# Five heads to two loads: K and V rows of 160 tokens in an eight-megabyte ring, against rows of 128 tokens for two heads

## The chip, the cores and the metric

The kernel runs on one core of one Trainium2 chip. The metric is the device time of that core in microseconds, the median of several executions. TensorE is called PE, VectorE DVE, ScalarE ACT, GpSimd POOL and SyncE SP, as in the profile; PEld is PE's weight load. SP issues the loads.

## The reference

Two attention blocks, A and B, each decode one token for a batch of 2 with 32 heads of 192 dimensions over a cache of 8192 tokens:

```python
q = (x @ wq).reshape(B, Sq, Hq, Dh).transpose(0, 2, 1, 3)     # x: 2 x 1 x 640, wq: 640 x 6144
scores = jnp.einsum("bhqd,bhkd->bhqk", q, k) * (Dh ** -0.5)   # k: 2 x 32 x 8192 x 192
p = _softmax(scores, axis=-1)
o = jnp.einsum("bhqk,bhkd->bhqd", p, v_cache)
out = o.transpose(0, 2, 1, 3).reshape(B, Sq, Hq * Dh) @ wo    # wo: 6144 x 640
```

All tensors are bf16; the two results are concatenated. K and V of both blocks are 805 MB, the four weights 31 MB.

## The kernel before

A load of K or V brings 128 partitions of 128 tokens (49152 B each, 6144 KB in all). As a head has 8192 tokens, that is two heads: partitions 0 to 63 hold one, 64 to 127 the other. The 2 x 32 heads of a block make 32 such pairs, the two blocks `NP = 64` steps. `rings` holds three loads; K and V go through the three slots in turn (order K V K V), V of a step one step behind K.

SP (`program_sync`, L92 to L159) loads the query weights of both blocks into slots 0 and 1 and the first K into slot 2, then one K when the projection of block A is done (`pr`), one V when that of B is, and from there one load after the other. Each waits for an earlier load of its kind to have landed and for PE to have used up what lies in its slot (`pv` counts value matmuls, `su` score matmuls). `hold` (L82) is a wait and an increment of a counter that nothing reads. At the end it loads the output weights of A, the last V in two halves, and the output weights of B in five pieces as PE frees their rows (`ca`).

PE (L316 to L421) first projects x (`pe_first`, L395 to L419): 12 column tiles of 512 per block, two to a turn, ten matmuls; ACT copies each result to `qrow` (L278). `make_q` (L322) spreads a pair's query over all partitions through a selection matrix, and ACT copies the right half for the lower and the upper 64 partitions into `qt` (L272, L273). In the main loop (L356) each step t does: `make_q` for the next pair; the scores of pair t; `put`, which lays a finished head's output into its column of `oall` (L327); the sum of the exponentials (L379); the value matmuls of pair t-1 in four turns of 16 (L385). After the last pair but for its values, the output rows of A are computed (`rows`, L339), then the last values, then the rows of B.

Scores: DVE multiplies K by the query in place, in four parts of 32 tokens (L241); PE adds up groups of 16 of the 192 products by matmuls with the identity (48 per pair, 12 per part, L370); DVE adds the 16 sums that remain (L246) and takes the maxima of the two halves (L250, L251); POOL spreads the maxima over partitions (L191); ACT makes the bias (L296), exponentials and their sums (L302). `closing` (L222) on DVE and `gather` on ACT (L286) scale the output of the step before.

## Time and profile before

| | |
|---|---|
| time, median of 3 | 1935.83 us (1935.47 to 1935.84) |
| profiled execution, span from first to last instruction | 1934.3 us; its own time outside the span is not recorded, and the median lies 1.5 us above the span |
| bytes read | 836.77 MB, 433 GB/s over the span |
| busy: PE, DVE, ACT, POOL | 1558.2, 1075.6, 186.5, 27.9 us |
| granted clock of PE, mean | 0.965 |
| K or V load, issue to landing, median | 26.5 to 26.8 us |

The busy share of an engine is over the whole span. A PE row's duration is that of pipelined matmuls, so the starts of rows say more than their lengths. "<-issue" behind a row is time in which the engine waited for its own instruction stream and for nothing that the profile shows. In a timeline row stand the start, the length, the engine, the line, the operation with its tiles, the count of merged instructions, and in brackets the idle time before it with what ended it.

### The profile page before, as it was taken

What the parts mean: (1) busy time and instruction counts of PE and PEld (TensorE: products, weight loads), DVE (VectorE), ACT (ScalarE), POOL (GpSimd) and SP (SyncE); (2) the same over time, 40 slices, a digit from 0 to 9 for tenths busy, and PEclk for the clock granted to TensorE, in tenths of its full rate; (3) what the DMA queues carried; (4) which work ended last, traced back from release to release, by engine and by line L of the source; (5) the groups of instructions that cost most, each with busy time, mean ns of one, the idle gap of its engine ahead of it and who ended that gap; (6) DMA issues with size and microseconds to landing.
All of it is one profiled execution on the core that took longest, in us unless ns stands there. A gap on an engine that the chain in (4) does not pass through costs nothing.

```text
span 1934.3 us, 31141 instructions
## 1 busy us (share of the span) xinstructions
PE 1558.2 (81%) x7939; PEld 743.0 (38%) x7939; DVE 1075.6 (56%) x717; ACT 186.5 (10%) x598; POOL 27.9 (1%) x83
## 2 busy tenths in 40 slices
PE   5787888887888887888887888887888888888887
PEld 1343333333333333333333333333433333433434
DVE  0665565565565565565565565565565565565560
ACT  2110010010010010010010010010010010010010
POOL 1000000000000000000000000000000000000000
PEclk9899999999999999999999999999999999999999
DMA  9999999999999999999999999999999999999999
GB/s 421 425 439 439 423 439 439 425 437 439 430 432 439 431 431 439 433 429 439 435 427 439 437 425 439 437 425 439 437 425 439 439 425 437 439 430 432 439 435 394
DMA packets 19896, 836.78 MB, mean 433 GB/s; under 512 B 2220, under 2 KB 2360, under 8 KB 2744
## 3 DMA queue, kind: packets, MB, share of 16 engines
q1 hardware_dynamic: 19880, 836.78, 100.0%
q10 hardware_dynamic: 16, 0.01, 0.0%
HBM read 836.77 MB, written 0.01 MB: 433 GB/s over the span
## 4 chain that ended last, share of the span: by engine, by line
DMA 44%; PE 32%; DVE 10%; issue 10%; another core or an unknown queue 2%; DVEq 1%; SPq 0%; ACT 0%; POOLq 0%
DMA rings<-in_B_k_cache_dram 22%; DMA rings<-in_A_k_cache_dram 19%; PE ops L385 18%; PE scps L370 12%; DVE rings L241 10%; DMA rings<-in_A_wo_dram 2%; DMA rings<-in_B_wo_dram 1%; DVEq L241 1%; PE oall L327 0%; PE qps L339 0%; PE ops L379 0%; SPq L102 0%; DVE qrow L212 0%; DVE sc L246 0%
## 5 line engine op out<-in xcount | busy, mean ns | idle before, releaser
L241 DVE TENSOR_TENSOR rings<-rings,qt 128x6144 bf16 x256 | 842.5, 3353 | 722.9 <-DMA rings<-in_B_k_cache_dram 351.0
L385 PE MATMUL ops<-rings,pb 128*34 x4096 | 712.9, 327 | 166.9 <-issue 166.9
L370 PE MATMUL scps<-rings,ident 128*128 x3072 | 749.0, 403 | 105.5 <-DVE rings L241 102.6
L385 PEld LDWEIGHTS ops<-rings,pb 128*34 x4096 | 381.3, 93 | 483.0 <-issue 233.5
L370 PEld LDWEIGHTS scps<-rings,ident 128*128 128x128 bf16 x3072 | 314.5, 102 | 524.0 <-issue 249.6
L246 DVE TENSOR_REDUCE sc<-scps 128x64 f32<-128x1024 f32 x128 | 155.5, 1215 | 81.4 <-PE scps L370 81.4
L286 ACT ACTIVATE oodd<-ops 2x192 f32<-2x192 f32 x65 | 20.9, 321 | 731.4 <-PE ops L385 731.4
L272 ACT ACTIVATE qt<-qps 64x192 bf16<-64x192 f32 x65 | 21.0, 323 | 650.1 <-DVE rings L241 649.6
L302 ACT ACTIVATE pb<-sc,nb 64x128 bf16<-64x128 f32 x128 | 82.4, 644 | 2.6
L322 PE MATMUL qps<-qrow,sel 36*128 (+1 forms) x66 | 21.8, 331 | 72.4 <-issue 69.6
L296 ACT ACTIVATE nb<-mg 64x1 f32<-64x1 f32 x128 | 25.7, 201 | 302.8 <-POOL mg L191 302.1
L191 POOL PARTITION_ALL_REDUCE mg<-mp x64 | 22.7, 354 | 1856.8 <-DVE mp L251 1856.8
L322 PEld LDWEIGHTS qps<-qrow,sel 36*128 (+1 forms) x66 | 6.1, 93 | 94.0 <-issue 94.0
L302 ACT ACTIVATION_READ_ACCUMULATOR pb<-sc,nb 64x1 f32 x128 | 39.2, 306 | 0.0
L411 PE MATMUL scps<-rings,xT 128*4 x120 | 29.4, 410 | 6.3 <-POOLq L188 6.3
L224 DVE RECIPROCAL rc<-ops 2x1 f32<-2x1 f32 x66 | 9.8, 149 | 34.5 <-PE ops L385 34.5
L327 PEld LDWEIGHTS oall<-on,place 2*128 x260 | 12.5, 92 | 29.7 <-issue 29.2
L226 DVE TENSOR_TENSOR oodd<-ops,oodd 2x192 f32<-2x192 f32 x66 | 21.5, 326 | 0.4 <-ACT oodd L286 0.4
L229 DVE TENSOR_SCALAR on<-oodd,rc 2x192 bf16<-2x192 f32 x66 | 20.3, 307 | 2.3
L273 ACT ACTIVATE qt<-qps 64x192 bf16<-64x192 f32 x65 | 21.1, 325 | 0.8
L327 PE MATMUL oall<-on,place 2*128 2x48 bf16 x260 | 19.6, 183 | 1.9 <-DVE on L229 1.7
L411 PEld LDWEIGHTS scps<-rings,xT 128*4 128x4 bf16 x120 | 10.7, 89 | 24.2 <-issue 12.2
(38 smaller groups left out, 109.9 us busy)
## 6 DMA issues: line engine op xcount, KB each, us to landing
rings<-in_A_k_cache_dram SPq DMA_DIRECT2D x32, 6144.0 KB, 26.8
rings<-in_A_v_cache_dram SPq DMA_DIRECT2D x32, 6144.0 KB, 26.5
rings<-in_B_k_cache_dram SPq DMA_DIRECT2D x32, 6144.0 KB, 26.7
rings<-in_B_v_cache_dram SPq DMA_DIRECT2D x31, 6144.0 KB, 26.6
rings<-in_B_wq_dram SPq DMA_DIRECT2D x1, 7680.0 KB, 37.9
rings<-in_A_wo_dram SPq DMA_DIRECT2D x1, 7680.0 KB, 30.7
rings<-in_A_wq_dram SPq DMA_DIRECT2D x1, 7296.0 KB, 20.2
rings<-in_B_v_cache_dram SPq DMA_DIRECT2D x2, 3072.0 KB, 26.8
```

Of the source, the lines that this page charges most:

```text
L191: eng.partition_all_reduce(mg[:], mp[:], 128, bass.bass_isa.ReduceOp.max).then_inc(Z["ar"], 1)
L226: eng.tensor_tensor(oodd[:], ops[0:2, 0:Dh], oodd[:], ALU.add).then_inc(Z["dd"], 1)
L241: eng.tensor_tensor(k3, k3, q3, ALU.mult).then_inc(Z["mu"], 1)
L246: eng.tensor_reduce(sc[:, h * 2 * TQ:(h + 1) * 2 * TQ], scps[:, 2 * h:2 * h + 2, :].rearrange("p k (t g) -> p (k t) g", g=DG), AXL.X, ALU. ...
L273: eng.activation(qt[64:128, :], qps[64:128, Dh:2 * Dh], ACTF.Identity).then_inc(Z["qtd"], 1)
L296: ins = eng.activation(nb[p0:p0 + 64, :], mg[p0:p0 + 64, h:h + 1], ACTF.Identity, scale=-scale)
L302: ins = eng.activation(pb[p0:p0 + 64, :, h::32], sc[p0:p0 + 64, :].rearrange("p (j a) -> p j a", a=2), ACTF.Exp, bias=nb[p0:p0 + 64, :], s ...
L322: eng.matmul(qps[:, 0:2 * Dh], sel[:].rearrange("p s m -> p (s m)")[:, bass.ds(k, 128)], qrow[:, bass.ds(c, 2 * Dh)], start=True, stop=Tru ...
L327: ins = eng.matmul(oflat[:, bass.ds(sec, WR)], place[:, bass.ds(at - a, 128)], on[:, a * WR:(a + 1) * WR], start=False, stop=False, skip_g ...
L370: ins = eng.matmul(dst, ident[:], src[:, :, 0:DG], start=(j == 0), stop=(j == NJ - 1))
L385: ins = eng.matmul(ops[0:PW, 0:2 * Dh], pbflat[:, bass.ds(aj + j * PW, PW)], rings[:, bass.ds(vj + j * (2 * Dh), 2 * Dh)], start=False, st ...
L411: ins = eng.matmul(scflat[0:4, bass.ds(to + h * QC, QC)], xT[:, c, :], rings[:, bass.ds(at + (c * N + h * QC), QC)], start=(c == 0), stop= ...
```

## The change

A chunk is now 32 tokens of 192, 12288 B, and a partition's row is five chunks of one load (160 tokens, 61440 B). Two loads (K0, K1) hold the keys of five heads, two more (V0, V1) the values, so head boundaries fall inside a load, at other partitions and chunks than before. A block has 12 groups of five heads and one of four, whose rows are 128 tokens (four chunks); 26 groups in all, 104 loads. The ring still has three slots, now of 61440 B per partition. The order is K0 of group t, V0 of group t-1, K1 of t, V1 of t-1. Before the first V come three K loads. Each load waits for the load two places ahead to have landed and for the load three places ahead to have been used up.

As one partition can belong to different heads in different chunks, a load needs up to three query vectors per partition (`qt` has 2 x 3). ACT no longer copies the queries: DVE makes them from `qps` with masks (`low`, `high`, `take`: 24 operations per group, of 192 or 96 columns, the first of each target a product with a mask column, the others a product added to it). The projection runs in turns of one column tile, five matmuls, 14 turns per block, and both blocks are projected before the first query is made. The maximum is taken per chunk, masked per head (`MN`), spread by POOL as five columns, and turned into biases on DVE. The exponentials are up to 18 operations per group in place of two per pair. POOL forwards the landings of loads to DVE (`kd`) and PE (`vs`). Reductions now run once per load over 2560 columns. PE's score loop has a turn per chunk; `put` has a loop of two turns for the two batch rows; values take five turns of 16 matmuls per load (four in the small group). At the end both V loads of the last group, the second in two halves, stand behind the output weights of A.

The added lines, cut to the core (removed ones stand in the kernel above; indentation shortened):

```diff
+    TC = 32
+    CW = TC * Dh
+    NCH = 5
+    SCH = 4
+    HCH = Sk // TC
+    T = NCH * TC
+    NS = 5
+    GB = B * Hn // NS
+    GL = GB + 1
+    NG = NBLK * GL
+    UR = 128 * NCH
...
+    load("k", 0, 0, NCH, 2 * SW, "k0")
+    eng.wait_ge(Z["pr"], NPD)
+    load("k", 0, UR, NCH, 0, "lb")
+    eng.wait_ge(Z["pr"], 2 * NPD)
+    def step(t, kb, krow, kn, ku, vb, vrow, vn, vu):
+        val = (lambda x: x) if isinstance(t, int) else eng.snap
+        first = isinstance(t, int) and t == 1
+        s0, s1, s2 = val(t % 3 * SW), val((t + 1) % 3 * SW), val((t + 2) % 3 * SW)
+        if not first:
+            hold(eng, "la", val(t * 32 - 32))
+            hold(eng, "pv", val(t * 2))
+        load("k", kb, krow, kn, s0, "la")
+        hold(eng, "lb", val(t * 32 - 16))
+        hold(eng, "su", NCH if first else val(t * (2 * NCH)))
+        load("v", vb, vrow, vn, s1, "lb")
+        hold(eng, "la", val(t * 32 - 16))
+        if first:
+            hold(eng, "su", 2 * NCH)
         else:
+            hold(eng, "pv", val(t * 2 + 1))
+        load("k", kb, val(krow + ku), kn, s2, "la")
+        hold(eng, "lb", val(t * 32))
+        hold(eng, "su", val(t * (2 * NCH) + NCH))
+        load("v", vb, val(vrow + vu), vn, s0, "lb")
+    def both(t, blk, g):
+        step(t, blk, eng.snap(g * GR), NCH, UR, blk, eng.snap(g * GR - GR), NCH, UR)
+    step(1, 0, GR, NCH, UR, 0, 0, NCH, UR)
+    with eng.Fori(2, GB) as t:
+        both(t, 0, t)
+    step(GB, 0, GB * GR, SCH, SR, 0, (GB - 1) * GR, NCH, UR)
+    step(GL, 1, 0, NCH, UR, 0, GB * GR, SCH, SR)
+    with eng.Fori(GL + 1, NG - 1) as t:
+        both(t, 1, eng.snap(t - GL))
+    step(NG - 1, 1, GB * GR, SCH, SR, 1, (GB - 1) * GR, NCH, UR)
...
+            hold(eng, "lb", 32 * g + 16)
+            eng.wait_ge(Z["su"], 2 * NCH * (g + 1))
+            load("v", 1, GB * GR, SCH, 0, "lb")
+            eng.wait_ge(Z["pv"], 2 * g + 3)
+            src = rows_of("v", 1, GB * GR + SR, SCH)
+            for h, (a, e) in enumerate(((0, LATE * CW), (LATE * CW, SCH * CW))):
+                eng.dma_start(rings[:, SW + a:SW + e], src[:, a:e]).then_inc(vq[h], 16)
...
+    pass_on("k0", 16, "kd")
+    pass_on("lb", 16, "kd")
+    maximum(1)
+    with eng.Fori(1, NG) as t:
+        pass_on("la", eng.snap(t * 32 - 16), "kd")
+        pass_on("lb", eng.snap(t * 32), "vs")
+        pass_on("la", eng.snap(t * 32), "kd")
+        pass_on("lb", eng.snap(t * 32 + 16), "vs")
+        maximum(eng.snap(t + 1))
...
+    def multiply(at, u, c):
+        v = max(0, min(2, c - 2 * u))
+        k3 = rings[:, bass.ds(at + c * CW, CW)].rearrange("p (t d) -> p t d", d=Dh)
+        q3 = qt[:, u, v, :].unsqueeze(1).broadcast_to([128, TC, Dh])
+        eng.tensor_tensor(k3, k3, q3, ALU.mult).then_inc(Z["mu"], 1)
+    def reduce(u, upto):
+        eng.wait_ge(Z["su"], upto)
+        eng.tensor_reduce(sc[:, u, :], scps[:].rearrange("p k (t g) -> p (k t) g", g=DG),
+                          AXL.X, ALU.add).then_inc(Z["re"], 1)
+    def take(u, s, d0, d1, at, new):
+        for v in range(3):
+            dst, src, m = qt[:, u, v, d0:d1], qps[:, at:at + d1 - d0], QW[:, (u * 3 + v) * 3 + s:(u * 3 + v) * 3 + s + 1]
+            if new:
+                ins = eng.tensor_scalar(dst, src, m, None, ALU.mult)
+            else:
+                ins = eng.scalar_tensor_tensor(dst, src, m, dst, ALU.mult, ALU.add)
+        return ins
+    def low(n, w):
+        val = (lambda x: x) if isinstance(n, int) else eng.snap
+        H = Dh // 2
...
+        eng.wait_ge(Z["qk"], val(n * 2 + 1))
+        eng.wait_ge(Z["qc"], val(n * 5 + 1))
+        take(0, 0, 0, Dh, 0, True)
+        take(1, 0, 0, H, 2 * Dh, True).then_inc(Z["qc"], 1)
+        eng.wait_ge(Z["qc"], val(n * 5 + 2))
+        take(0, 1, 0, Dh, Dh, False).then_inc(Z["qc"], 1)
+        eng.wait_ge(Z["qc"], val(n * 5 + 3))
+        take(0, 2, 0, H, 2 * Dh, False).then_inc(Z["qs"], 1)
+    def high(n):
+        H = Dh // 2
+        eng.wait_ge(Z["qk"], eng.snap(n * 2 + 2))
+        eng.wait_ge(Z["qs"], eng.snap(n + 1))
+        take(1, 0, H, Dh, 0, True)
+        take(0, 2, H, Dh, 0, False).then_inc(Z["qc"], 1)
+        eng.wait_ge(Z["qc"], eng.snap(n * 5 + 4))
+        take(1, 1, 0, Dh, H, False).then_inc(Z["qc"], 1)
+        eng.wait_ge(Z["qc"], eng.snap(n * 5 + 5))
+        take(1, 2, 0, Dh, H + Dh, False).then_inc(Z["qt"], 1)
+        eng.wait_ge(Z["qt"], eng.snap(n + 1))
+    low(0, 0)
+    with eng.Fori(0, NG) as t:
+        y = eng.snap((t + 31) >> 5)
+        at = [eng.snap((t + 2 - y * 2) % 3 * SW), eng.snap((t + 3 - y) % 3 * SW)]
+        w = eng.snap(kind(t))
+        high(t)
+        eng.wait_ge(Z["kd"], eng.snap(t * 2 + 1))
+        for c in range(NCH):
+            multiply(at[0], 0, c)
+        closing(t - 2)
+        eng.wait_ge(Z["ex"], eng.snap(t * 2 + 1))
+        reduce(0, eng.snap(t * (2 * NCH) + NCH))
+        n = eng.snap(t * 4)
+        last = sc[:, 0, SCH * TC:T]
+        eng.wait_ge(Z["re"], eng.snap(t * 2 + 2))
+        eng.tensor_scalar(last, last, flag[:, bass.ds(w, 1)], None, ALU.min).then_inc(Z["ch"], 1)
+        eng.wait_ge(Z["kd"], eng.snap(t * 2 + 2))
+        for c in range(NCH):
+            multiply(at[1], 1, c)
+        low(eng.snap(t + 1), eng.snap(kind(t + 1)))
+        reduce(1, eng.snap(t * (2 * NCH) + 2 * NCH))
+        eng.wait_ge(Z["ch"], eng.snap(n + 1))
+        eng.wait_ge(Z["re"], eng.snap(t * 2 + 3))
+        eng.tensor_reduce(cm, sc[:].rearrange("p u (c t) -> p (u c) t", t=TC), AXL.X,
+                          ALU.max).then_inc(Z["ch"], 1)
...
+        eng.tensor_reduce(mp, nb[:], AXL.X, ALU.max).then_inc(Z["mx"], 1)
+        eng.wait_ge(Z["ar"], eng.snap(t + 1))
+        eng.scalar_tensor_tensor(nb[:], mg.unsqueeze(2).broadcast_to([128, NS, 2 * NCH]), -scale, mask,
+                                 ALU.mult, ALU.add).then_inc(Z["nbd"], 1)
+        eng.sem_inc(Z["ch"], 1)
...
+    def exps(u):
+        for v, (c0, c1) in enumerate(SPANS[u]):
...
+                ins = eng.activation(dst, src, ACTF.Exp, bias=nb[:, s, k:k + 1], scale=scale,
+                                     accum_out=rs[:, u, v, s:s + 1])
         ins.then_inc(Z["ex"], 1)
+    with eng.Fori(0, NG) as t:
+        eng.wait_ge(Z["nbd"], eng.snap(t + 1))
+        eng.wait_ge(Z["pv"], eng.snap(t * 2 + 2))
+        exps(0)
+        gather(t - 1)
+        exps(1)
...
+    def put(t):
+        z = eng.snap((t + 17) >> 5)
+        x = nc.snap(z * (4 * 65) - t * (4 * NS) + (P0 + 2 * 4 * NS), min_val=3, max_val=PLW - 256)
+        z = eng.snap(z * 128)
+        with eng.Fori(0, B) as b:
+            zb, xb = eng.snap(b * 64 + z), eng.snap(b * 128 + x)
+            for a in range(4):
+                ins = eng.matmul(oall[:, bass.ds(zb, WR)], place[:, bass.ds(xb - a, 128)],
+                                 on[:, a * WR:(a + 1) * WR], start=False, stop=False,
+                                 skip_group_check=True)
+            ins.then_inc(Z["pl"], 1)
...
+        with eng.Fori(eng.snap(p * NG), eng.snap(p * 2 + NG)) as t:
+            with eng.Fori(0, 2) as u:
+                with eng.If(t < NG):
+                    y = eng.snap((t + 31) >> 5)
+                    k_at = eng.snap((t + 2 - y * 2 + u + y * u) % 3 * T)
+                    n = eng.snap(t * (2 * NCH) + u * NCH + 1)
+                    hold(eng, "re", eng.snap(t * 2 + u + 1))
+                    with eng.Fori(0, NCH) as c:
+                        at, to = eng.snap(c * TC + k_at), eng.snap(c * 512)
+                        eng.wait_ge(Z["mu"], eng.snap(n + c))
+                        dst = scflat[:, bass.ds(to, 512)].rearrange("p (t g) -> p t g", g=DG)
                         for j in range(NJ):
+                            ins = eng.matmul(dst, ident[:], ringt[:, bass.ds(at, TC), j * DG:(j + 1) * DG],
+                                             start=(j == 0), stop=(j == NJ - 1))
+                        ins.then_inc(Z["su"], 1)
+                    h = eng.snap(t * NS + (128 + NS) - ((t + 20) >> 5))
+                    eng.wait_ge(Z["qs"], eng.snap(t + u + 1))
+                    make_q(eng.snap(((h >> 5) & 3) * 128), nc.snap((h & 31) * Dh + u * HQ, min_val=0, max_val=QW0 - HQ))
+                with eng.If(t > 0):
+                    with eng.If(u < 1):
+                        hold(eng, "on", eng.snap(t + 1))
+                        put(t)
+                        blank(ops[0:PW, 500:501], PW, True)
+                        eng.wait_ge(Z["ex"], eng.snap(t * 2 + 1))
+                        for k in range(6):
+                            eng.matmul(ops[0:NS, 448:449], rs[:, k // 3, k % 3, :], ones, start=False, stop=False,
+                                       skip_group_check=True)
+                    with eng.If(t < NG + 1):
+                        n2 = nc.snap(kind(t + GL - 1) * -1 + NCH, min_val=SCH, max_val=NCH)
+                        lu = eng.snap(late * u)
+                        v_at = eng.snap((t + 1 - u + lu) % 3 * SW)
+                        pat = eng.snap(u * PU)
+                        w = eng.snap(t * 2 + u)
+                        hold(eng, "vs", w)
+                        with eng.Fori(0, n2) as g:
+                            eng.wait_ge(Z["vh"], eng.snap((g & lu) + 1))
+                            aj, vj = eng.snap(g * (PG * 16) + pat), eng.snap(g * (PG * 2 * Dh) + v_at)
+                            for j in range(PG):
+                                eng.matmul(ops[0:PW, 0:2 * Dh],
+                                           pbflat[:, bass.ds(aj + (j // 4 * 64 + j % 4 * 8), PW)],
+                                           rings[:, bass.ds(vj + j * (2 * Dh), 2 * Dh)], start=False, stop=False,
+                                           skip_group_check=True)
+                        blank(ops[0:PW, 500:501], PW, False).then_inc(Z["pv"], 1)
...
+            with eng.Fori(0, NPD) as t:
                 eng.wait_ge(Z["wq"], b)
+                eng.wait_ge(Z["qe"], eng.snap(k * NPD + t + 1))
+                z = eng.snap((t + 4) >> 4)
+                to, at = eng.snap((t & 1) * QC), nc.snap(k * SW + t * QC - z * N - ((t + 3) >> 4) * QO, min_val=0, max_val=SW + N - QC)
+                for c in range(DC):
+                    ins = eng.matmul(scflat[0:4, bass.ds(to, QC)], xT[:, c, bass.ds(z, 4)],
+                                     rings[:, bass.ds(at + c * N, QC)],
+                                     start=(c == 0), stop=(c == DC - 1))
                 ins.then_inc(Z["pr"], 1)
+        eng.wait_ge(Z["qe"], 2 * NPD + 2)
+        for u in range(2):
+            eng.wait_ge(Z["dv" if not u else "qs"], 2 - u)
+            eng.matmul(qps[:, 0:HQ], sel[:, 0, :], qrow[:, u * HQ:(u + 1) * HQ],
+                       start=True, stop=True).then_inc(Z["qk"], 1)
```

More of the change, by code (lines that the diff above doesn't have):

```diff
@@ L55, in build_kernel @@
+        qt = sb("qt", [128, 2, 3, Dh], BF16)
+        small = sb("small", [128, 32], F32)
+        rs = sb("rs", [128, 2, 3, NS], F32)
+        nb = sb("nb", [128, NS, 2 * NCH], F32)
+        oodd = sb("oodd", [NS, Dh], F32)
+        on = sb("on", [NS, Dh], BF16)
         ident = sb("ident", [128, 128], BF16)
[L56 to L57 removed]
+        sel = sb("sel", [36, NBLK * B, 128], BF16)
         oallS = sb("oallS", [128, WR, B], BF16)
[L59 removed]
@@ L60, in build_kernel @@
-        warm = sb("warm", [128, 2], F32)
-        sb("pad", [128, 1648], BF16)
+        xo = sb("xo", [36, D], BF16)
+        xT = sb("xT", [128, DC, 8], BF16)
         rings = sb("rings", [128, 3 * SW], BF16)
-        qrow = sb("qrow", [36, N], BF16)
-        pb = sb("pb", [128, T // 2, PW], BF16)
-        sel = sb("sel", [36, NBLK * B, 128], BF16)
-        out_sb = [sb(f"out_sb{k}", [PW, NH2], BF16) for k in range(NBLK)]
-        scps = ps("scps", [128, 4, 512], F32)
+        qrow = sb("qrow", [36, QW0], BF16)
@@ L179, in program_pool @@
-            eng.wait_ge(Z["init"], 5)
-            eng.affine_select(out=place[:], in_=place[:], compare_op=ALU.is_equal, fill=0.0, base=-128,
-                              pattern=[[1, 264]], channel_multiplier=-4)
-            eng.memset(ones[:], 1.0)
+                only(sel[:, k, :], ALU.is_equal, 0.0, -(34 * (k // B) + k % B), [[0, 128]], 1)
+            for tile, pat, ch in kinds:
+                only(tile, ALU.is_ge, 0.0, 0, pat, ch)
+            for tile, at, ns, pat, ch in bounds:
+                ins = only(tile, ALU.is_ge, NEG, -HCH * at, [[-HCH, ns]] + pat, ch)
```

369 lines of the change are left out of this document (145 added, 224 removed).

## Prediction

> **What bounds the kernel now.** I read the page first, then the DMA view of two stretches, then the timeline of one steady pair of heads, of the first 130 us and of the last 70 us.
>
> ```profile
> DMA  9999999999999999999999999999999999999999
> ...
> q1 hardware_dynamic: 19880, 836.78, 100.0%
> ```
>
> The page's slices: the 16 DMA engines are never idle, from the first slice to the last. So the time is the time of the bytes, and any moment in which the queue runs dry is added to it. The DMA view of 400 to 1800 us (K and V rows of 49152 B) and of 22 to 38 us (rows of 61440 B of the query weights) prices a packet:
>
> ```profile
> DMA packets 13906, 607.23 MB, mean 434 GB/s; under 512 B 1552, under 2 KB 1552, under 8 KB 1552
> ...
> q1 hardware_dynamic: 13906, 607.23, 100.2%
> ```
> ```profile
> DMA packets 112, 6.88 MB, mean 430 GB/s; under 512 B 0, under 2 KB 0, under 8 KB 0
> ...
> q1 hardware_dynamic: 112, 6.88, 99.3%
> ```
>
> Without the 1552 tiny ones, 12354 packets share 1.002 x 16 x 1400 us: 1.817 us each. The 112 long ones share 0.993 x 16 x 16 us: 2.270 us. The ratio is 1.249 and that of the bytes 1.250: a longer row buys between nothing and 0.1%. The steady state:
>
> ```profile
> 404.59 0.34 SPq L102 DMA_DIRECT2D rings<-in_A_v_cache_dram  x1
> ...
> 417.12 13.16 DVE L241 TENSOR_TENSOR rings<-rings,qt 128x6144 bf16 x4 [11.05 <-DMA rings<-in_A_k_cache_dram]
> ...
> 418.90 0.34 SPq L102 DMA_DIRECT2D rings<-in_A_k_cache_dram  x1
> ...
> 446.10 13.17 DVE L241 TENSOR_TENSOR rings<-rings,qt 128x6144 bf16 x4 [10.90 <-DMA rings<-in_A_k_cache_dram]
> ...
> 462.24 1.23 DVE L246 TENSOR_REDUCE sc<-scps 128x64 f32<-128x1024 f32 x1 [1.18 <-PE scps L370]
> ...
> 463.33 1.99 PE L385 MATMUL ops<-rings,pb 128*34 x11 [0.57 <-issue]
> ```
> ```profile
> 1867.12 13.16 DVE L241 TENSOR_TENSOR rings<-rings,qt 128x6144 bf16 x4 [11.05 <-DMA rings<-in_B_k_cache_dram]
> ```
>
> From 417.12 to 1867.12 lie 50 pairs (K and V of two heads): 29.00 us each, 14.50 per load, and VectorE waits 11 us of each for its K. A load is issued when the third-last has been used up, some 12 us before the one in flight lands. That lead is the cover. PE's own pace shows where a late start let data pile up:
>
> ```profile
> 101.17 2.82 PE L385 MATMUL ops<-rings,pb 128*34 x16 [0.66 <-issue]
> 105.08 0.33 PE L322 MATMUL qps<-qrow,sel 36*128 x1 [1.08 <-issue]
> 105.98 10.53 PE L370 MATMUL scps<-rings,ident 128*128 x48 [0.57 <-issue]
> ...
> 126.20 2.81 PE L385 MATMUL ops<-rings,pb 128*34 x16 [0.67 <-issue]
> ```
> ```profile
> 434.35 2.77 PE L385 MATMUL ops<-rings,pb 128*34 x16 [0.61 <-issue]
> ...
> 437.78 2.48 PEld L385 LDWEIGHTS ops<-rings,pb 128*34 x16 [1.02 <-issue]
> 437.79 2.78 PE L385 MATMUL ops<-rings,pb 128*34 x16 [0.67 <-issue]
> ```
>
> A pair can pass in 126.20 - 101.17 = 25.0 us. Twelve score matmuls (one chunk of 32 tokens) take 10.53/4 = 2.63 us; a turn of 16 value matmuls takes 437.79 - 434.35 = 3.44, of which 0.97 to 1.02 is the turn of the loop itself, and each matmul inside needs 2.48/16 = 0.155 us to be issued.
>
> **The change part by part.** I write K0 K1 V0 V1 for the four loads of a group of five heads.
>
> *Bytes.* They stay. 24 groups of four long loads and two of four short ones replace 128 loads. A long load takes 14.50 x 1.25 = 18.1 us, a group 72.5. By the packet ratio the stream saves 0 to 2 us; I take 1.
>
> *The steady state.* VectorE per group: ten multiplications of 3.29 (13.16/4), two reductions, and 24 scaled query copies: under 55 us of 72.5, so the masks are hidden under waits for K; without that cover they cost their 7 us per group. PE: 10 chunks x 2.63 + 10 turns x 3.44 = 60.7, and four passages. Before, values to scores is 105.98 - 103.99 = 2.0 us and scores to values 463.33 - 462.24 = 1.1. If the four stay so, the group needs 66 us; if each score chunk also pays the 0.67 us of idle that a value turn shows and each passage grows by the second turn of the placing loop (four matmuls and a loop turn, about 1.2) and as much register work, it needs 77. I take 71.5: 2.3 us for each way in, 2.5 and 5.5 for the ways out (the second holds both turns of `put`), less the two last loop turns. That is nearest to the sum of what is listed. 71.5 is under 72.5, so the loads still set the pace, but with 1 us to spare, where before it was 4 in 29.
>
> The Trainium skill ("TensorE: Matmul & The Clock Gate", Part 1) says that an idle window of about 3.4 us drops PE to half clock until a busy one has passed. This trace agrees so far (busy times, granted clock, DMA share and GB/s of four microseconds):
>
> ```profile
> 420.00:424.00 4.00, 2.88 (x9) 1.24 (x10) 4.00 (x3) 0.19 (x2) 0.00 (x0) 0.72 0.91 393
> ```
>
> The granted clock is 0.72 in those 4 us. The new 5.5 us passage could call it in every group; that is at most 1.7 us of PE, and would speak for the first rival below.
>
> *The start.* Here the order K K K V K V matters, with VectorE's start:
>
> ```profile
> 22.15 14.91 PE L411 MATMUL scps<-rings,xT 128*4 x60 [4.80 <-POOLq L188]
> ...
> 40.24 14.45 PE L411 MATMUL scps<-rings,xT 128*4 x60 [1.48 <-POOLq L188]
> ...
> 55.12 13.16 DVE L241 TENSOR_TENSOR rings<-rings,qt 128x6144 bf16 x4 [49.14 <-DVEq L232]
> ```
> ```profile
> 30.81 1.01 ACT L278 ACTIVATE qrow<-scps  x1 [1.14 <-PE scps L411]
> 32.97 1.01 ACT L278 ACTIVATE qrow<-scps  x1 [1.15 <-PE scps L411]
> ```
>
> The projection goes from 6 turns of ten matmuls (2.16 us each, 32.97 - 30.81) to 14 turns of five. A turn costs at least half of 2.16, at most all of it. By the issue row it is 1.0 + 5 x 0.155 = 1.8, and it computes more addresses: I take 1.9, so 26.6 us a block. Before, the first head's query was made between the two blocks; now after both: 22.15 + 26.6 + 0.5 + 26.6 = 75.9. Then the last copy (0.6, between the 0.32 of 192 columns and the 1.01 of 1024, and 0.2 of hand-over), a query matmul (0.5), twelve masked copies, a second query matmul (0.4), twelve more.
>
> ```profile
> L246 DVE TENSOR_REDUCE sc<-scps 128x64 f32<-128x1024 f32 x128 | 155.5, 1215 | 81.4 <-PE scps L370 81.4
> ...
> L272 ACT ACTIVATE qt<-qps 64x192 bf16<-64x192 f32 x65 | 21.0, 323 | 650.1 <-DVE rings L241 649.6
> ```
> ```profile
> 430.28 0.33 DVE L226 TENSOR_TENSOR oodd<-ops,oodd 2x192 f32<-2x192 f32 x1
> ...
> 430.64 0.31 DVE L229 TENSOR_SCALAR on<-oodd,rc 2x192 bf16<-2x192 f32 x1
> ```
> ```profile
> 405.79 0.28 DVE L251 TENSOR_REDUCE mp<-sc 64x1 f32<-64x128 f32 x1
> 406.28 0.35 POOL L191 PARTITION_ALL_REDUCE mg<-mp  x1 [28.52 <-DVE mp L251]
> 406.67 0.41 ACT L296 ACTIVATE nb<-mg 64x1 f32<-64x1 f32 x2 [4.62 <-POOL mg L191]
> ```
>
> A masked copy is 0.31 to 0.33 for 192 columns and some 0.21 for 96; twelve with their waits are 3.5 to 3.6 us. So the first multiplication starts at M = 75.9 + 0.8 + 0.5 + 3.5 + 0.4 + 3.6 = 84.7, where it started at 55.1. Bounds: M = 64 with turns of 1.08 (the second block cannot begin before 40.2), 92 with turns of 2.16.
>
> From M on it is a chain. Five multiplications 16.45; scores end 2.95 after the last (446.10 + 13.17 = 459.27 to 462.24, less 0.05): M + 19.4. Reduction of 2560 columns 2.8 (1.215 for 1024 and 0.28 for 128 give the slope): M + 22.4. K1: scores end at M + 41.9. The next query half hides; reduction, maxima (1.2), the all-reduce (406.67 - 406.07 = 0.6), bias and the second half of the query, 3.6: K0 of group 1 starts at M + 50.8, scores end at M + 70.2. Only then comes V0 of group 0: passage 5.5, five turns 16.6: M + 92.4. The seventh big load, K0 of group 2, waits for that buffer, behind it on SP all other loads. It moves about 1.1 us after its issue:
>
> ```profile
> rings<-in_A_wq_dram SPq DMA_DIRECT2D x1, 384.0 KB, 3.5
> ```
>
> (384 KB need 0.9 us of moving; the other 2.6 bound the lead from above, 0 from below.) So it moves at M + 93.7. Fed without a break it would move at 39.7 + 6 x 18.1 = 148.4, since the second block's weights have landed when PE starts at 40.24. The queue lacks M + 93.7 - 148.4 = 30 us (9 to 37 over the bounds of M). After that the same sums give each load 1.5 to 5 us of lead.
>
> *The end.* Before:
>
> ```profile
> 1899.37 6.68 PE L339 MATMUL qps<-rings,oallS 128*2 128x320 bf16 x96 [1.81 <-POOLq L196]
> ...
> 1907.75 2.77 PE L385 MATMUL ops<-rings,pb 128*34 x16 [0.62 <-issue]
> ...
> 1918.15 2.77 PE L385 MATMUL ops<-rings,pb 128*34 x16 [0.69 <-issue]
> ...
> 1922.61 0.57 PE L327 MATMUL oall<-on,place 2*128 2x48 bf16 x4 [1.69 <-DVE on L229]
> 1923.73 8.72 PE L339 MATMUL qps<-rings,oallS 128*2 128x320 bf16 x96 [0.55 <-ACT oallS L207]
> ```
> ```profile
> 1932.50 0.43 ACT L312 ACTIVATE out_sb<-qps 34x320 bf16<-34x320 f32 x1 [9.00 <-PE qps L339]
> ```
>
> One value load stands behind the first block's output rows, and the last rows (8.72 instead of 6.68) still wait for their weights: the last K lands at 1867.1, four loads later (14.5 + 18.1 + 14.5 + 18.1) it is 1932.3, and the span ends 2.0 us after. Now two value loads stand there. With X the landing of the last K, the bytes end at X + 18.1 + 18.1 + 14.5 + 14.5 + 18.1 = X + 83.3 and the span could end at X + 85.3. PE: K0's scores end at X - 13.2 (it landed at X - 32.6), V0 of group 24 at X + 8.9, the last scores at X + 24.3, V1 at X + 43, output rows X + 44.9 to X + 51.6, passage 5, four turns, passage 3, four turns (13.2 each): X + 86; closing and placing 4.3 (before 1923.73 - 1920.92 = 2.8), rows 6.7, copy and store 1.8: X + 98.7. PE ends 13 us later than the bytes allow (6, were PE never late, to 20, were it a passage later each time).
>
> *Sum*, against this execution's span: 1934.3 - 1 + 30 + 13 = 1976 us. The median is 1.5 us above that span, so **1978 us**.
>
> **The rivals.**
>
> 1. *PE becomes the bound* (72.5 us per group is the point). For it: the spare of 1 us and the granted clock of 0.72 after idle time; against: 71.5. At 74.5 it costs 2 us in each of 22 groups, less 3 us of lead, and leaves PE some 8 us later at the end: 1978 + 49 = 2027 us.
>
> 2. *The larger buffers cover start and end* (not slower). Each buffer may be used up to 36.3 us after its landing instead of 29.0; if that holds the queue full as now, only the packets' 1 us remains: 1935 us. It decides where K0 of group 2 is issued by 148 us, which needs M below 55. Against it: K0 alone lands at 57.8, and M cannot be under 64 by the bounds above.
>
> 3. *A load has a price of its own* (faster). 24 loads fewer would then save up to 2.6 us each, 62 us: 1978 - 62 = 1916. Against it: eight packets of 1.817 are 14.53, and a load takes 14.50; nothing is left for a fixed part, because the next load is always in flight. The Trainium skill ("DMA: Bandwidth & Descriptors", Anatomy of one DMA) gives about 2.0 us of fixed cost per DMA; by that it would be 48 us and 1930. The 3.5 us of the small load agrees with such a cost, the steady period shows it hidden.
>
> 4. *The start is short*: turns at PE's pace, M = 64, gap 9, end 6 to 13: 1950 us.
>
> **How the numbers follow.** The forecast has 0.62, PE as the bound 0.18, the short start 0.08, the cover 0.08, a price per load 0.04. About 0.2% (4 us) is what a measurement of this kernel can tell from no change. Slower: 0.62 + 0.18 + 0.08 = 0.88; same 0.08; faster 0.04. The forecast's own range is 1950 to 1995; the whole one takes in part of the first rival: 1948 to 2012.
>
> **What would show it.** Start: DMA slices below 9 between 95 and 180 us, the first multiplication near 85 us, projection turns near 1.9 us; with turns near 1.1 the start is sized wrong. Steady: K0 starts every 72.5 us with VectorE waiting for DMA; a longer period, with VectorE waiting for nothing from DMA, is rival 1. End: the last output rows in 6.7 us without waits for weights; if they wait, the end costs nothing. A period under 72.4 or a packet under 2.26 us would overturn the price of the bytes.

## The result and the profile after

The changed kernel takes 2035.21 us (median of 5, 2033.9 to 2035.47), the kernel before 1935.83: a ratio of 1.051 (95% interval 1.05 to 1.0523). It is slower, as forecast, but by 99 us where 42 were forecast, and outside the range of 1948 to 2012. The profiled execution's span is 2034.2 us, against 1976 in the sum. One of the five executions of the kernel before took 3037.29 us, which nothing here explains, and no comparison uses it.

The page of the changed kernel: DMA busy share in 40 slices, the queue's share, the chain that ended last; and the chain of the kernel before.

```profile
DMA  9867999999999999999999999999999999999994
...
q1 hardware_dynamic: 16424, 836.77, 96.1%
...
PE 55%; DMA 18%; issue 16%; DVE 10%; DVEq 1%; SPq 0%; ACT 0%; POOL 0%; POOLq 0%; ACTq 0%
```
```profile
DMA 44%; PE 32%; DVE 10%; issue 10%; another core or an unknown queue 2%; DVEq 1%; SPq 0%; ACT 0%; POOLq 0%
```

The DMA dips appear where they were expected, at the start and in the last slice. But the chain has also changed hands: PE and issuing now hold 71% of it, DMA 18%. SP's waits (what it waited for, total us, times, longest), after and before, say the same:

```profile
SPq L105 <- PE ops L440: 653.1, 48, 21.8
SPq L105 <- PE scps L497: 620.6, 51, 29.7
SPq L105 <- DMA rings<-in_B_k_cache_dram: 175.7, 25, 9.8
```
```profile
SPq L84 <- DMA rings<-in_A_v_cache_dram: 375.4, 32, 12.2
...
SPq L84 <- PE scps L370: 129.8, 62, 6.4
```

Before, the waits in the load loop were mostly for landings (1418 us over the four tensors, against 241 for PE); now they are mostly for PE to use up a buffer (1274 us, against 473 for landings). Three stretches of the timeline show it. The start (last projection turns, the first multiplication, K0 of group 2, its multiplication):

```profile
79.71 1.24 PE L550 MATMUL scps<-rings,xT 128*4 x5 [0.92 <-issue]
...
81.87 1.24 PE L550 MATMUL scps<-rings,xT 128*4 x5 [0.92 <-issue]
...
93.33 16.43 DVE L306 TENSOR_TENSOR rings<-rings,qt 128x6144 bf16 x5 [0.57 <-DVE qt L319]
...
189.51 0.36 SPq L124 DMA_DIRECT2D rings<-in_A_k_cache_dram  x1
...
213.83 6.63 DVE L306 TENSOR_TENSOR rings<-rings,qt 128x6144 bf16 x2 [0.55 <-DVE qt L319]
```

A projection turn takes 81.87 - 79.71 = 2.16 us, 1.24 of it in its five matmuls. M, the first multiplication, is at 93.3, and K0 of group 2 is issued at 189.5. The steady state (K0 multiplications of groups 5 and 10, and value turns and a K1 multiplication between):

```profile
433.37 13.16 DVE L306 TENSOR_TENSOR rings<-rings,qt 128x6144 bf16 x4 [0.54 <-DVE qt L319]
...
579.73 2.48 PEld L523 LDWEIGHTS ops<-rings,pb 128*37 x16 [1.28 <-issue]
579.76 2.77 PE L523 MATMUL ops<-rings,pb 128*37 x16 [0.98 <-issue]
583.42 2.49 PEld L523 LDWEIGHTS ops<-rings,pb 128*37 x16 [1.22 <-issue]
583.46 2.78 PE L523 MATMUL ops<-rings,pb 128*37 x16 [0.93 <-issue]
...
613.41 16.43 DVE L306 TENSOR_TENSOR rings<-rings,qt 128x6144 bf16 x5 [4.35 <-POOLq L246]
...
629.96 13.53 PE L497 MATMUL scps<-rings,ident 128*128 x60 [1.73 <-DVE rings L306]
...
799.40 13.16 DVE L306 TENSOR_TENSOR rings<-rings,qt 128x6144 bf16 x4 [0.55 <-DVE qt L319]
```

(799.40 - 433.37) / 5 = 73.2 us per group, and K0 is multiplied right after VectorE's own query copies, with no wait for DMA. K1 does still wait for its landing, 4.35 us in this row (through POOL, which passes the landings on). That wait does not reach PE: K1's five multiplications start at 613.4, PE takes up its scores only at 630.0, and it stands idle there for 1.73 us, as it does before other scores without such a wait (1.78 in the row of 1940.49 below). A value turn is 583.46 - 579.76 = 3.70 us. The end:

```profile
1920.51 3.36 DVE L306 TENSOR_TENSOR rings<-rings,qt 128x6144 bf16 x1 [0.93 <-POOLq L246]
...
1940.49 13.53 PE L497 MATMUL scps<-rings,ident 128*128 x60 [1.78 <-issue]
...
2016.03 0.17 PE L440 MATMUL ops<-ident 128*37 128x1 bf16 x1
...
2022.90 9.47 PE L467 MATMUL qps<-rings,oallS 128*2 128x320 bf16 x96 [2.03 <-issue]
```

X, the multiplication of the last K, is at 1920.5; the span ends 113.7 us later. No row after X waits for DMA.

These marks divide the excess. By the forecast's own working a fed queue ends at 1934.3 - 1 = 1933.3, so X would be 1933.3 - 85.3 = 1848.0, and K0 of group 2 would land at 148.4 + 18.1 = 166.5. Against that:

| | forecast | measured |
|---|---|---|
| start: multiplication of K0 of group 2, against 166.5 | 30 | 213.8 - 166.5 = 47 |
| from there to X, against 1848.0 | 0 | 1920.5 - 1848.0 - 47.3 = 25 |
| end: X to the end, against 85.3 | 13 | 113.7 - 85.3 = 28 |
| sum | 43 | 100 |

### The profile page after: what moved, and what is told of

The parts are those of the page before. It is cut to its first block, busy times and chain, and to the rows that moved or that the text cites. A ratio compares the mean times of both kernels' runs of the same rounds, so it can differ in the third digit from the quotient of the medians.

```text
span 2034.2 us, 33460 instructions
## 1 busy us (share of the span) xinstructions
PE 1602.8 (79%) x8226; PEld 786.9 (39%) x8226; DVE 1251.0 (61%) x1197; ACT 194.6 (10%) x998; POOL 18.0 (1%) x59
## 2 busy tenths in 40 slices
DMA packets 16444, 836.81 MB, mean 411 GB/s; under 512 B 1836, under 2 KB 1976, under 8 KB 2360
## 4 chain that ended last, share of the span: by engine, by line
PE 55%; DMA 18%; issue 16%; DVE 10%; DVEq 1%; SPq 0%; ACT 0%; POOL 0%; POOLq 0%; ACTq 0%
PE ops L523 26%; PE scps L497 25%; DMA rings<-in_B_k_cache_dram 9%; DVE rings L306 9%; DMA rings<-in_A_k_cache_dram 7%; DMA rings<-in_B_wq_dram 2%; PE scps L550 1%; PE qps L467 1%; PE oall L455 1%; PE qps L444 1%; DVE qt L319 1%; DVE sc L310 0%; DVEq L306 0%; DVE qt L317 0%; PE ops L510 0%
## 5 line engine op out<-in xcount | busy, mean ns | idle before, releaser
L523 PE MATMUL ops<-rings,pb 128*37 x4096 | 764.8, 345 | 220.7 <-issue 220.5
L497 PE MATMUL scps<-rings,ident 128*128 x3120 | 721.8, 388 | 127.5 <-issue 86.8
L523 PEld LDWEIGHTS ops<-rings,pb 128*37 x4096 | 416.1, 102 | 562.3 <-issue 336.5
L310 DVE TENSOR_REDUCE sc<-scps 128x160 f32<-128x2560 f32 x52 | 146.9, 2824 | 465.4 <-PE scps L497 465.4
L417 ACT ACTIVATE pb<-sc,nb 128x32 bf16<-128x32 f32 (+1 forms) x468 | 168.8, 562 | 1436.8 <-DVE nb L381 1436.8
L417 ACT ACTIVATION_READ_ACCUMULATOR pb<-sc,nb 128x1 f32 x468 | 131.9, 317 | 0.0
L319 DVE SCALAR_TENSOR_TENSOR qt<-qps,QW,qt 128x192 bf16<-128x192 f32 (+1 forms) x396 | 124.8, 371 | 3.8
L317 DVE TENSOR_SCALAR qt<-qps,QW 128x96 bf16<-128x96 f32 (+1 forms) x240 | 67.0, 345 | 88.2 <-PE qps L557 75.9
L550 PE MATMUL scps<-rings,xT 128*4 x140 | 38.6, 413 | 26.6 <-issue 24.3
L455 PE MATMUL oall<-on,place 5*128 5x48 bf16 x216 | 28.2, 190 | 27.7 <-issue 27.7
L444 PE MATMUL qps<-qrow,sel 36*128 x52 | 19.4, 373 | 1.1 <-DVE qt L319 1.1
```

The costliest lines, as they stand in the source:

```text
L310: eng.tensor_reduce(sc[:, u, :], scps[:].rearrange("p k (t g) -> p (k t) g", g=DG), AXL.X, ALU.add).then_inc(Z["re"], 1)
L317: ins = eng.tensor_scalar(dst, src, m, None, ALU.mult)
L319: ins = eng.scalar_tensor_tensor(dst, src, m, dst, ALU.mult, ALU.add)
L417: ins = eng.activation(dst, src, ACTF.Exp, bias=nb[:, s, k:k + 1], scale=scale, accum_out=rs[:, u, v, s:s + 1])
L444: eng.matmul(qps[:, 0:HQ], sel[:].rearrange("p s m -> p (s m)")[:, bass.ds(row, 128)], qrow[:, col if not isinstance(col, int) else slice( ...
L455: ins = eng.matmul(oall[:, bass.ds(zb, WR)], place[:, bass.ds(xb - a, 128)], on[:, a * WR:(a + 1) * WR], start=False, stop=False, skip_gro ...
```

## The experiments

The edits are shown shortened. The theory after the result: PE, not the loads, sets the pace (73.2 us where the loads could 72.5), mostly by loop turns; the late first multiplication is passed on whole; the end is PE's queue of work. The rivals: long rows are slow by themselves; the masks on VectorE cost; the three buffers are what starves the start.

**Values written out.**

```diff
-with eng.Fori(0, n2) as g:       # turns of 16 matmuls
+values(0, 2 * PG)                # the same matmuls in a row
+values(2 * PG, SCH * PG)
+with eng.If(n2 > SCH):
+    values(SCH * PG, NCH * PG)
```

> The changed kernel with the value loop written out: the 80 (64) value matmuls of a half group follow each other without the loop's turns. Theory (PE sets the pace): a turn of 16 costs 3.71 us now and about 16 x 0.155 = 2.5 without the loop, so PE needs some 12 us less per group, 61 instead of 73.2; the loads set the pace again, K0 multiplications 72.5 us apart, the block boundary costs nothing. 24 x 0.7 us, 8 at the boundary, some 5 at the start and 13 turns x 1.2 at the end are won: 1991 us (1983 to 2000). Rival (the loads themselves take 73.2 us a group, because the queue restarts badly with long rows): the period stays 73.2 and only start and end gain, 2014 us.

Measured 1981.14 us (1981.03 to 1982.22): 54 us won, 10 more than expected and just below the range. Its K0 multiplications of groups 5 and 10, and its SP waits:

```profile
424.76 6.63 DVE L306 TENSOR_TENSOR rings<-rings,qt 128x6144 bf16 x2 [7.35 <-POOLq L246]
...
787.04 6.63 DVE L306 TENSOR_TENSOR rings<-rings,qt 128x6144 bf16 x2 [7.36 <-POOLq L246]
```
```profile
SPq L105 <- DMA rings<-in_B_k_cache_dram: 364.1, 25, 15.4
...
SPq L105 <- PE scps L497: 205.4, 51, 29.8
```

362.28 / 5 = 72.46: the loads' price to 0.1%, and VectorE (through POOL) and SP wait for landings again. The bytes of 300 us (400 to 700 us) say it without any chain; the DMA view of the changed kernel, then of this one:

```profile
DMA packets 2353, 128.84 MB, mean 429 GB/s; under 512 B 256, under 2 KB 256, under 8 KB 256
...
q1 hardware_dynamic: 2353, 128.84, 99.9%
```
```profile
DMA packets 2396, 130.50 MB, mean 435 GB/s; under 512 B 272, under 2 KB 272, under 8 KB 272
```

So the long rows are not slow, and a busy share of 99.9% hid a queue that was 1.3% short of bytes. X comes at 1888.3, so 40 us remain ahead of it and 1979.6 - 1888.3 - 85.3 = 6 behind it. What went with the loop is a turn's branch, its wait and its two address computations together; no run separates them.

**Masks.** One scaled copy instead of three for each slice, and all chunks of a load multiplied by the first of the three query vectors (the tokens of the other heads then get a wrong query):

```diff
-for v in range(3):
+for v in range(1):
```

> The changed kernel without the masks: each slice of a query is scaled once instead of three times (8 copies per group instead of 24), and all five chunks of a half group are multiplied by the first of the three query tiles; the rows that hold tokens of two heads are then computed with the wrong query, all else is as before. Theory (VectorE is not the bound; the masks are on the path only before the first multiplications): the first multiplication 5 us earlier, a few us more in the chain of the first two groups, the steady period stays 73.2 us: 2026 to 2031 us. Rival (the masked copies lengthen each group): 16 copies x 0.35 = 5.6 us less per group, the loads' 72.5 us set the pace: 2005 to 2015 us.

Measured 2027.64 us (2025.91 to 2027.87). The first multiplication is at 88.66, 4.7 us earlier:

```profile
88.66 16.43 DVE L306 TENSOR_TENSOR rings<-rings,qt 128x6144 bf16 x5 [0.57 <-DVE qt L319]
```

The masks cost 7.6 us, all of it at the start: K0 of group 2 comes 9.6 us earlier, X 8.3, and a group still takes (789.80 - 423.81) / 5 = 73.2 us. They are no part of the steady state, as the forecast had it.

**PE's cost, put to the test with more work.** Twelve one-column matmuls behind each half group's values, first with fixed operands, then with an address from a register:

```diff
+for k in range(12):
+    blank(ops[0:PW, 500:501], PW, False)
```
```diff
+for k in range(12):
+    eng.matmul(ops[0:PW, 500:501], ident[:, 0:PW], rings[:, bass.ds(v_at + k, 1)], ...)
```

> The changed kernel with 12 more matmuls of one column behind the values of each half group, about 0.16 us each: 2.0 us of PE per half, 4.0 per group. Theory (PE sets the pace at 73.2 us with no slack): the period becomes 77.2 us, the time rises by 4.0 in each of 25 groups plus the end, 2135 us (2115 to 2145). Rival (the loads set the pace and PE has about 1 us to spare): the period becomes 76.2 us, 2110 us; with more slack than 4 us only start and end grow, 2041 us.

> The changed kernel with 12 more one-column matmuls behind each half group's values, as in the run of 2040.2 us, but with an address that comes out of a register. Theory (PE sets the pace, and what it pays for is the computed address, 0.155 us each, not the matmul): 1.9 us per half, 3.7 per group, so the period goes from 73.2 to 76.9 us and the time to 2130 us (2110 to 2140). Rival (PE has slack, or the matmuls themselves are hidden): 2040 us as with fixed addresses.

The first took 2040.18 us (2039.73 to 2040.45), the second 2130.69 (2130.24 to 2131.15). By the expectation the first result spoke for slack in PE; the trace shows that the work added was next to no work (13 matmuls in 0.47 us), a group still takes 73.3 us, and the profiled span is 1.3 us longer:

```profile
590.06 0.47 PE L440 MATMUL ops<-ident 128*37 128x1 bf16 x13
```

The second version cost what it should (its matmuls, and K0 of groups 5 and 11):

```profile
447.44 16.43 DVE L306 TENSOR_TENSOR rings<-rings,qt 128x6144 bf16 x5 [0.54 <-DVE qt L319]
456.64 1.57 PE L528 MATMUL ops<-rings,ident 128*37 x12 [0.23 <-issue]
...
908.35 16.43 DVE L306 TENSOR_TENSOR rings<-rings,qt 128x6144 bf16 x5 [0.55 <-DVE qt L319]
```

(908.35 - 447.44) / 6 = 76.8 us per group, 3.6 more. The two differ in the moving operand alone: a fixed column of `ident`, or columns of `rings` at a computed address. So in the changed kernel PE has no slack in which to hide 1.8 us more per half group, and what it pays for is most likely the computed address; a fixed address in `rings` was not run.

**The start.** Two tiles to a projection turn:

```diff
-with eng.Fori(0, NPD) as t:
+with eng.Fori(0, NPD // 2) as t2:
+    for h in range(2):           # t = 2 * t2 + h, four banks instead of two
```

> The changed kernel with the projection in 7 turns of two tiles (ten matmuls) for each block instead of 14 turns of one; nothing else. Theory (the late first multiplication is passed on one for one): a turn of two tiles takes 2.6 to 3.4 us where two of one take 4.3, so the first multiplication comes at 70 to 81 us instead of 93.3 and the whole is 12 to 24 us shorter: 2011 to 2023 us; the steady period stays 73.2 us and the stretch after the last K stays 114 us. Rival (the start is made up for later, or other work sets it): 2035 us, no change.

Measured 2026.82 us (2023.68 to 2027.67). The turn was mis-sized: 3.73 us for two tiles, not 2.6 to 3.4. Five matmuls take 1.24 us, as before; between the two tiles lie 0.27 us and between turns 0.99. The first multiplication moved from 93.33 to 85.29, the median time by 8.4: one for one, within executions that lie 4 us apart.

Then the projection written out with fixed addresses, beside the written-out values; and also the first query between the two projections:

```diff
-with eng.Fori(0, NBLK) as k:
-    with eng.Fori(0, NPD) as t:
+for k in range(NBLK):
+    for t in range(NPD):
```
```diff
+    if not k:
+        eng.wait_ge(Z["qe"], NPD + 2)
+        ...                      # the two matmuls of the first query, moved here
```

> The changed kernel with two things written out: the value loop, as in the run of 1981.1 us, and the projection (28 tiles with fixed addresses instead of 2 x 14 loop turns). Theory (the late first multiplication is what the start costs, and it is passed on one for one): a tile takes 1.1 to 1.3 us instead of 2.16, the first multiplication comes at 65 to 70 us instead of 93, that of K1 26 us earlier (23 to 28): 1955 us (1950 to 1962). Rival (something else holds the first loads back, such as the three buffers): less than half of that, 1968 us or more.

> As the kernel with values and projection written out, and the first query made between the projections of the two blocks, as the kernel before had it. Theory: the first multiplication then waits for the landing of K0 alone, near 58 us, K1 is multiplied some 35 us earlier than at 117, nearly all of the start is won: 1946 us (1940 to 1952), of which some 6 us stand at the end and the rest at the start. Rival (long rows or the order K V K V cost something that has not been named): it stays above 1955 us.

Measured 1959.73 us (1958.53 to 1960.39) for the first, with its first multiplication at 68.7 and 35.29 / 28 = 1.26 us for a tile: as expected. The second took 1956.81 (1956.09 to 1957.42), above its range; by its text the rival held. Its trace names what was missing:

```profile
59.62 16.43 DVE L306 TENSOR_TENSOR rings<-rings,qt 128x6144 bf16 x5 [8.31 <-POOLq L246]
...
69.33 15.87 PE L497 MATMUL scps<-rings,ident 128*128 x60 [3.41 <-issue]
...
89.06 16.43 DVE L306 TENSOR_TENSOR rings<-rings,qt 128x6144 bf16 x5 [0.49 <-issue]
```
```profile
1898.26 1.52 PE L467 MATMUL qps<-rings,oallS 128*2 128x320 bf16 x20
1903.94 7.00 PE L467 MATMUL qps<-rings,oallS 128*2 128x320 bf16 x76 [4.15 <-issue]
```

The first multiplication does wait for the landing of K0, at 59.6, but PE is still projecting block B and begins the scores at 69.3, so K1 is multiplied at 89.1, 28 us earlier than in the changed kernel and not 35. And within the first block's rows PE stands still for 4.15 us with nothing to wait for. These 7 and 4 us add up to the 11 by which it lies above the expected 1946. The first comes from PE's own order of work, not from the length of the rows; what makes PE stand still was not tested. X is at 1860.9: 13 us remain ahead of it and 1955.2 - 1860.9 - 85.3 = 9 behind it.

The fourth corner, the repaired start with the value loop as it was:

> The changed kernel with the projection written out and the first query made between the two projections; the value loop keeps its turns, so PE stays at 73.2 us a group. With the kernel that has neither (2035.2), that with written-out values alone (1981.1) and that with all three (1956.8) it fills a table of two by two. Theory (while PE sets the pace, the lateness of the start is passed on whole): the multiplication of K1 came 28.0 us earlier (89.06 instead of 117.08) with all three, so 2035.2 - 28 = 2007 us (2003 to 2012), the period stays 73.2 and the stretch after the last K 114 us. Rival (start and pace only add up as they did under a fed queue): 2035.2 - 24.3 = 2011 us; (PE's lag grows again to what it was): 2030 us or more.

Measured 2008.43 us (2006.92 to 2010.56). K0 of groups 5 and 11:

```profile
404.93 6.62 DVE L306 TENSOR_TENSOR rings<-rings,qt 128x6144 bf16 x2 [0.54 <-DVE qt L319]
```
```profile
844.09 16.43 DVE L306 TENSOR_TENSOR rings<-rings,qt 128x6144 bf16 x5 [0.54 <-DVE qt L319]
```

439.16 / 6 = 73.2 again, and X is at 1891.9, the end 113.3 us later:

| | value loop in turns | values written out |
|---|---|---|
| start as changed | 2035.2 | 1981.1 |
| start repaired | 2008.4 | 1956.8 |

Start and pace are two causes that nearly add up: 27 and 54 us alone, 78 together. None of these beats the kernel before, and by the forecast's working none could by more than a few us: the bytes alone need 1933.

**Lateness alone, in the kernel before.** Its first multiplication waits for V of the first pair:

```diff
+eng.wait_ge(Z["vs"], 16)
```

> The kernel before (rows of 128 tokens), its first multiplication held until V of the first pair has landed, some 83.5 us instead of 55.1; nothing else. Theory (what the start costs is the lateness, not the rows): K of the third pair is issued 17 us after the first multiplication, the queue runs dry for about 18 us and then for 3 more; PE's pace cannot win back bytes: 1957 us (1952 to 1963). Rival (the lead of the two loads in flight covers it): 1936 to 1940 us.

Measured 1961.42 us (1961.32 to 1961.92), 25.7 above the kernel before on the same chip:

```profile
83.98 13.16 DVE L242 TENSOR_TENSOR rings<-rings,qt 128x6144 bf16 x4 [78.00 <-DMA rings<-in_A_v_cache_dram]
...
101.48 0.36 SPq L102 DMA_DIRECT2D rings<-in_A_k_cache_dram  x1
...
120.82 0.35 SPq L102 DMA_DIRECT2D rings<-in_A_v_cache_dram  x1
```

With short rows, too, a first multiplication 28.9 us late costs nearly all of its lateness: the queue is dry from the landing at 84 to 101, and again before 121. The lead of the loads in flight covers 3 us, not 29.

**The end.** Each block keeps 5 of its 48 output rows:

```diff
+if r < at + n - 1:
+    continue
```

> The changed kernel with 38 of the 48 row matmul pairs... that is 43 of 48 rows of the output weights left out in each block (the loads stay): the output lacks their part. Theory (after the last K, PE's work sets the end and the bytes wait for it): the first block's rows take 0.7 us instead of 6.7, the last 1.0 instead of 9.5, so the end comes 14 us earlier, 2021 us (2018 to 2024). Rival (the last weights' landing sets the end): their loads are issued 6 us earlier, and the last rows wait for them; no more than 6 us are won, 2029 us.

Measured 2029.64 us (2029.09 to 2030.08): 5.6 us, where 14 were expected, and by the total the rival holds. But this kernel's start differs, though no line of it was touched (projection turns, then X and the last copy):

```profile
73.33 0.59 ACT L404 ACTIVATE qrow<-scps  x1 [1.85 <-PE scps L551]
75.76 0.59 ACT L404 ACTIVATE qrow<-scps  x1 [1.85 <-PE scps L551]
...
1927.77 16.43 DVE L306 TENSOR_TENSOR rings<-rings,qt 128x6144 bf16 x5 [0.20 <-issue]
...
2026.55 0.43 ACT L434 ACTIVATE xo<-qps 34x320 bf16<-34x320 f32 x1 [4.08 <-PE qps L468]
```

A turn takes 2.43 us instead of 2.16, and X comes 7.3 us later. From X the span has 2028.3 - 1927.8 = 100.5 us instead of 113.7: 13.2 us won there, and the last rows wait for nothing. So the end is PE's by this stretch; the total is a mixture of two effects, one of them not intended and not explained.

## Why the prediction was right or wrong, step by step

- *The bytes.* Right. With PE out of the way a group takes 72.46 us against 72.5; a longer row buys nothing that can be measured. The four loads of a group are 32 packets, by the forecast's 2.27 us 72.6 us, so nothing of the 72.46 is left for a price per load, and rival 3 falls. The Trainium skill's fixed cost of about 2.0 us per DMA ("DMA: Bandwidth & Descriptors", Anatomy of one DMA), which that section gives for the GpSimd path while these loads are SP's, leaves no trace in that period. Rival 2, the cover, falls: K0 of group 2 was issued at 189.5, not by 148, and even with the first multiplication at 59.6 X came 13 us late. Rival 4 falls with M.
- *The masks.* Right: hidden in the steady state, on the path at the start.
- *PE at 71.5 us against 72.5: the step that failed.* It is 73.2. The turns were taken over from the old loop: 3.44 for a value turn, which is 3.70 to 3.71 (PEld idles 1.22 to 1.28 between turns instead of 0.97 to 1.02), and 2.63 for a score chunk, which is 13.53 / 5 = 2.71. The 16 value matmuls themselves take 2.77 to 2.82 us in both kernels, so the turn is longer by its idle time. What lengthened that stays open: both loops compute two addresses and one wait value in a turn, the new one with one addition more. Ten of each are 64 instead of 60.7; the four passages, which were estimated, came out 1.6 us smaller (73.2 - 64 = 9.2 instead of 10.8). The estimate was bounded by 66 and 77 and the point of decision stood at 72.5, within 1 us of the value taken: the weight of 0.62 on one side was not earned. Rival 1 is what happened, with a smaller price per group (0.7 us, not 2), so that its 2027 us comes near the result by luck: the rest came from start and end, and from where the forecast did not look. Around the change of blocks the loads get short, 4 chunks instead of 5, while PE still does the scores of five. The windows show it (busy times, granted clock, DMA share, GB/s):

```profile
940.00:1020.00 80.00, 63.97 (x334) 31.95 (x334) 52.83 (x61) 10.16 (x55) 0.73 (x2) 0.96 0.95 399
1020.00:1100.00 80.00, 63.73 (x330) 31.48 (x328) 58.22 (x49) 10.01 (x56) 0.37 (x1) 0.96 0.95 406
```

  Of the 25 us 12 are 16 full groups x 0.75 and 11 lie here: from K0 of group 11 to K0 of group 16 the changed kernel takes 1231.20 - 872.60 = 358.6 us, and 1207.32 - 859.50 = 347.8 with the values written out. The last 2 come with the last, small group.
- *The half clock.* It came, but its price of at most 1.7 us per group did not. Behind the passage the granted clock is 0.50, and the first three value turns still take (621.67 - 610.46) / 3 = 3.74 us, as the others do: what sets them is the issuing. The rule of the Trainium skill ("TensorE: Matmul & The Clock Gate", Part 1), as the forecast cites it, names an idle window of about 3.4 us. No idle time of that length stands in these rows: from the query matmul that ends at 606.0 to the drop (0.84 from 608 to 609, then 0.50) PE is never idle for more than 0.8 us at a time. In and just before the forecast's four microseconds, which it read as agreement, the longest is 1.21 us. So the trace agrees with the drop to half, not with what the rule says calls it.

```profile
610.50:615.50 5.00, 5.00 (x16) 2.44 (x17) 2.09 (x1) 0.00 (x0) 0.00 (x0) 0.50 0.91 393
```
```profile
610.46 10.43 PE L523 MATMUL ops<-rings,pb 128*37 x48 [1.33 <-issue]
...
621.67 2.80 PE L523 MATMUL ops<-rings,pb 128*37 x16 [0.79 <-issue]
```

- *The start: mechanism right, size wrong.* 47 us, not 30. M was 93.3, above even its upper bound of 92. 7.3 us are the projection turn: 2.16, the upper bound, where 1.9 was taken. Its idle time was sized well (0.92 where 1.0 was taken); its five matmuls take 1.24 us where 5 x 0.155 was taken, though the forecast's own row of 60 in 14.45 us gives 0.24 for each. 1.3 us are the first query's masked copies. From M to the issue of K0 of group 2 it was 96.2 us instead of 92.6: 2.5 of the difference lie ahead of K0 of group 1, which is multiplied at 146.66 = M + 53.3 instead of M + 50.8. K0 of group 2 landed 21.1 us after its issue by the DMA view, where 19.2 was taken, and then waited 3 us more for VectorE's chain. The claim that lateness is passed on whole nearly stood in each run: 8.0 us earlier won 8.4; K1 some 28 us earlier won 27 with the value loop in turns and 24 with it written out; 28.9 us later cost 25.7 in the kernel before.
- *The end: mechanism right, size wrong.* The weights never kept PE waiting, as forecast, but PE ended at X + 113.7, not X + 98.7. 9.2 us came with PE's lag: the last scores end at X + 33.5 instead of X + 24.3, since PE was at the values of V0 of group 24 until 1938.7. Closing and placing take 2022.90 - 2016.20 = 6.7 us instead of 4.3, and the last rows 9.5 instead of 6.7. These 2.8 us are no wait for weights: all bytes have landed (DMA share 0.00), and the granted clock starts at 0.50, where the first block's rows, 6.68 us long, had 1.00. Here, unlike in the value turns, half the clock did cost time. The forecast read the 8.72 us of these rows in the kernel before as a wait for weights; its trace shows 1.2 us of such waits there, and a clock of 0.50 in the first three microseconds. The changed kernel's last rows (busy times, granted clock, DMA share, GB/s):

```profile
2023.00:2026.00 3.00, 3.00 (x24) 1.43 (x22) 0.00 (x0) 0.00 (x0) 0.00 (x0) 0.50 0.00 0
```

So the sum failed at one estimate that decided who sets the pace. That error came back in the steady stretch and at the end; the start's excess is mostly sizes of its own.

## What to carry to other kernels

A time that is copied from one loop to another is an estimate, even where the matmuls in a turn are the same: here a turn cost about 1 us beside its matmuls, 0.26 us more than in the old loop, and over ten turns that was more than the whole spare. Where the estimate of one engine's period lies within its own uncertainty of another's, forecast the range over both sides: being second by 1 us in 72 is not a cover, and a stretch that has less to load than the average loses more, as around the change of blocks. A DMA share near 100% can hide a short queue; the bytes in a window do not.

## What the runs showed that had not been expected

- Thirteen matmuls of one column with fixed operands pass in 0.47 us; twelve with an address from a register take 1.57 and lengthen a half group by 1.8. So the cost is not the matmul; that it is the address is the likely reading, as said above.
- The same loop, in a kernel changed elsewhere, ran at 2.43 us per turn instead of 2.16, and the two kernels with both values and projection written out stood still for 3.74 and 4.15 us just behind the jump in the row code, where the changed kernel and those with only one of the two written out did not. The cause of both stays open; no run tested it.
- Writing out 52 half groups of value matmuls won 54 us, of which the steady pace is only 12; 7 are won by K0 of group 3, 11 around the change of blocks, 2 in the last small group and 22 behind X.
